# Batches 0 to 3 of an attention-and-MLP kernel: three W2 blocks cast into another tile, and sums, copies and transposes put at other places of the order

## The chip, the cores and the metric

One core of one Trainium2 chip runs the whole program. The metric is the device time of one execution in microseconds; each time is the median of several runs. Besides, one execution was taken by the hardware profiler. All times inside an execution are counted from its first instruction.

## The reference

Attention with 16 query heads over 4 key and value heads, then a residual block that mixes tokens and then channels:

```python
x  = softmax(q @ k.T / 8) @ v            # 8 batches, 16 heads, 384 tokens, 64 per head -> (8, 384, 1024)
u  = x + lam * (w_tok @ (alpha1 * x + beta1))
a2 = alpha2 * u + beta2
out = u + lam * (relu(a2 @ w_ch1) @ w_ch2)   # w_ch1 1024 x 4096, w_ch2 4096 x 1024
```

Inputs and output are float32; the kernel multiplies in bfloat16 and accumulates in float32.

## The kernel before

**Pairs.** The eight batches go through the two channel products in four pairs. Each product of a pair is done as a 2 x 2 block scheme with seven block products in place of eight, so blocks of W1, W2 and of the activations are first added or subtracted on VectorE (DVE). The operand sums of a2 lie in seven parts of one tile, `ops`; part k is `opb(k)`. Channel product one of the first pair is `first_product` (line 652, its matmuls are L692), channel product two is `second_product` (line 739, matmuls L763). The later pairs use the loops of `pair` (L842 for product one, L908 for product two).

**What sets the order.** The program is scheduled by hand: each engine executes its instructions in the order in which the Python code issues them, and so do the DMA queues of SyncE (SP) and GpSimd (POOL). A product is a generator; each `yield` ends a *step*. In product one a step is four matmuls of 384 columns, in product two four matmuls of 512 columns. The table `plan` (filled by `put(ps, second, step, function, ...)`) says which other work is issued after which step of which pair. Work that stands in the table at (0, 1, u) is issued at step u of the first pair's second product; by the count of weight loads on L763, step 8 of it begins at 137.4 us, step 23 at 155.3, step 36 at 171.4, step 40 at 176.8 and step 61 at 202.4.

**What runs beside.** While the first pair (batches 0 and 1) is in its second product, `side(2)` and `side(3)` do the attention of the next two batches: scores, exponentials, `av` (times v, divided by the sum), `tok_flip` (the token product L332, the addition L339 giving u in the tile `xr`, the product with alpha2 L342 giving a2 in one of five buffers in `obuf` that are used in turn), then `spill` (DMA of u to the output, L235) and the flip of a2 into `ops`. A *flip* is a transpose: for batch 2 `a2_transpose` (L345), a DMA transpose issued by SP into `opb(3)` or `opb(4)`; for batch 3 `turn`, on TensorE (PE) with a copy on ScalarE (ACT) into `opb(0)` or `opb(1)`. The q and k of the next batch are flipped by SP as well (L175, L171). Batches 0 and 1 go through the same stages before product one; the list near line 1182 is the end of that part, and the first steps of product one are among its entries.

**Product one of the first pair.** It goes over eight groups g in `order0` = 6, 7, 5, 4, 0, 1, 2, 3. Groups 6, 7 and 5 (`EARLY`) have a part of their products done during attention and run `SEQ0`; the others run `SEQ1`, fourteen steps (o, e) with o the block product and e one of two halves. The steps o = 1, 6, 5, 3 accumulate into the PSUM bank X[e]; after each of 1, 6, 5 an ACT copy (L700) takes a snapshot before PE adds the next. After (3, e) ACT copies a bias (L707), and DVE L709 reads the bank Y[t]; after that (4, e) may write Y[t], which L713 reads. DVE also makes the W1 sums of the next group in `sum_block` (L576 and L572), issued after four of the steps, and ACT runs `finish` (L662, a relu over the previous group's sums).

**W2 blocks.** W2 lies in quarters: "11", "12", "21", "22", each in four blocks c of 512 KB in bfloat16. A block is cast from float32 by a POOL DMA (L499); "21" is cast to DRAM and loaded by SP (L497). Blocks are held in a ring of six slots (`w1`), three slots in `pad`, or at `home(c)` in `arena`. `queue` is a list of loads; `pump` issues from its head whenever a slot comes free. After "21" is used (o = 2), its four slots take "22" c = 1 to 3 and, later, a second copy of "21" ("again") that is needed for o = 4; "again" c = 1 takes the slot of "22" c = 0 in `pad`. The first three W1 blocks of the next pair follow in the queue.

**Later pairs.** Their product one runs `SEQ1` in eight groups; `sum_w1` (L518, L523) makes the next group's sums after steps 2, 5, 8, 11.

Of the kernel before, what the change touches and what calls it, by code (L numbers as in the profile page):

```python
# [13 lines left out]
def kernel(  # L14
# [21 lines left out]
    nc = tc.nc  # L36
# [14 lines left out]
    NST = S // P  # L51
# [7 lines left out]
    RING = 6  # L59
# [63 lines left out]
    def by_tok(ap):  # L123
        return ap.rearrange("(p st) d -> p st d", st=NST)
# [97 lines left out]
    def side(b):  # L222
# [9 lines left out]
            return opb((3, 0)[b % 2] + p // 4)[:, p % 4]  # L232

        def spill(p):
            nc.sync.dma_start(out=by_tok(out[b])[:, :, cols(p)], in_=x_of(p))  # L235

        def cols(p):
            return slice(p * P, (p + 1) * P)
# [152 lines left out]
            flip(p)  # L391

        def flip(p):
            if not first:
                spill(p)
            if not by_pe(p):
                a2_transpose(p)

        def by_pe(p):
# [13 lines left out]
        at = {}  # L413
# [6 lines left out]
        for p in range(NP):  # L420
            put((4, 10, 14, 18, 24, 29, 33, 35)[p], av, p)
            put((8, 15, 17, 22, 27, 32, 36, 38 if b % 2 else 39)[p], tok_flip, p)
            if by_pe(p):
                put(((13, 20, 23, 28, 34, 37, 40, 42) if b == 3 else (0, 0, 0, 0, 0, 36, 39, 41))[p], turn, p)
        return at
# [61 lines left out]
        nc.gpsimd.dma_start(out=stored(c).rearrange("p (a c) -> p a c", a=4), in_=w2_block(name, c))  # L487

    def load_w2(name, c, slots=None):
        if slots is None:  # L490
            raw[name, c] = None, home(c)
        else:
            slot = slots.pop(0)
            raw[name, c] = slot, place(slot)
        at = raw[name, c][1]
        if name in ("21", "again"):
            nc.sync.dma_start(out=at, in_=stored(c))  # L497
        else:
            nc.gpsimd.dma_start(out=at.rearrange("p (a c) -> p a c", a=4), in_=w2_block(name, c))  # L499
# [82 lines left out]

    queue = [(load_block, kind, gp) for kind, gp in (("R1", 0), ("R2", 0), ("L1", 1), ("L2", 1), ("R1", 1), ("R2", 1))]
    queue += [(load_w2, "21", c, w1_free) for c in range(4)]
    for name, cs, slots in (("12", (0, 1), w1_free), ("12", (2, 3), pad_free), ("22", (0,), pad_free), ("22", (1, 2, 3), w1_free),
                            ("again", (0,), w1_free), ("again", (1,), pad_free), ("again", (2, 3), w1_free)):
        queue += [(load_w2, name, c, slots) for c in cs]
    queue += [(load_w1, c) for c in order1[:3]]
    for i in range(1, NB):
        heads = [(load_w1, c) for c in order1[:4]] if i + 1 < NB else []  # L590
        queue += [(load_w1, c) for c in order1[4:]] + [(fetch, i, n) for n in range(SLOTS - 2)] + heads[:2]
# [60 lines left out]
    def first_product(flush):  # L652
# [12 lines left out]
        for i, g in enumerate(order0):  # L665
            nxt = order0[i + 1] if i + 1 < len(order0) else None
            quick = g in EARLY
            snap, part_lo = {}, {}
            ts = slice(2 * g, 2 * g + 2)
            for k, (o, e) in enumerate((((7, 0), (7, 1)) if i == 0 else ()) + SEQ0 if quick else SEQ1):  # L670
                G = g
                if o == 8:
                    if nxt not in EARLY:
                        continue
                    o, G = 7, nxt
                t = 2 * G + e
                lo, hi = bias1[:, t:t + 1], bias1[:, NH + t:NH + t + 1]
                if i == 0 and (o, e) == (6, 0):
                    lead_banks.close()
                    share_banks("Z")  # L680
                if i == 0 and o == 7:
                    begin_x(t)
                if o == 1:
                    begin_x(t)
                if o == 7:
                    Ys[t] = bank([P, 512], "mm", "Y") if G == g else pairs["Z"].tile([P, 512], f32, tag="Z", name="Y", bufs=4)
                if o == 2:
                    Z = pairs["Z"].tile([P, 512], f32, tag="Z", name="Z", bufs=4)
                ps = X[e] if o in (1, 6, 5, 3) else Ys[t] if o in (7, 4) else Z
                n = S + (o in (1, 2, 5, 3))  # L690
                for dt in range(NDT // 2):
                    nc.tensor.matmul(out=ps[:, :n], lhsT=tb[G, o][:, dt, e * P:(e + 1) * P], rhs=opb(FIRST1[o], n)[:, dt],  # L692
                                     start=(o in (1, 2, 7) and dt == 0), stop=(dt == NDT // 2 - 1), skip_group_check=True)
                wide, ps = ps, ps[:, :S]
                if o in (1, 6, 5):
                    w = S + 2
                    q = ((2 if i % 2 else 8) + 2 * (1, 6, 5).index(o) + e) % 12 * w
                    n = S + (o == 1)
                    snap[o, e] = snaps[:, q:q + S]
                    nc.scalar.copy(out=snaps[:, q:q + n], in_=wide[:, :n])  # L700
                    if o == 1:
                        part_lo[e] = snaps[:, q + S:q + S + 1]
                elif o == 2:
                    tt(out=lo, in0=wide[:, S:S + 1], in1=part_lo[e], op=ADD)
                    stt(out=lead_hid[:, t, 0], in0=ps, scalar=lo, in1=snap[1, e], op0=ADD, op1=ADD)  # L705
                elif o == 3:
                    nc.scalar.copy(out=hi, in_=wide[:, S:S + 1])  # L707
                    nc.scalar.activation(out=lead_hid[:, t, 3], in_=ps, func=RELU, bias=hi)
                    stt(out=lead_hid[:, t, 1], in0=Ys[t][:, :S], scalar=hi, in1=snap[5, e], op0=ADD, op1=ADD)  # L709
                    if nxt in EARLY:  # L710
                        begin_x(2 * nxt + e)
                elif o == 4:
                    stt(out=lead_hid[:, t, 2], in0=ps, scalar=lo, in1=snap[6, e], op0=ADD, op1=ADD)  # L713
                if (o, e) in ((2, 1), (3, 1)) and i % 2:
                    free_blocks("L" if o == 2 else "R", g // 2)
                if (o, e) == (6, 0) and i == 0:
                    tt(out=opb(2), in0=opb(0), in1=opb(1), op=ADD)
                if (o, e) == (6, 1) and i == 0:
                    tt(out=opb(0), in0=opb(4), in1=opb(6), op=SUB)
                at = ((6, 0), (6, 1), (5, 0), (5, 1)) if quick else tuple(SEQ1[u] for u in (2, 5, 8, 11))  # L720
                if (o, e) in at and nxt is not None:
                    m = (5, 7, 6, 4)[at.index((o, e))]
                    sum_block(nxt, m)
                    if m == 4 and i == 0:
                        free_blocks("L", nxt // 2)
                if k == 1 and i:
                    finish(order0[i - 1])
                if (o, e) == (4, 0):
                    nc.scalar.activation(out=lead_hid[:, ts, 1], in_=lead_hid[:, ts, 1], func=RELU)
                if (o, e) == (4, 1):  # L730
                    nc.vector.tensor_scalar(out=lead_hid[:, ts, 2], in0=lead_hid[:, ts, 2], scalar1=0.0, scalar2=None,
                                            op0=mybir.AluOpType.max)
                    tt(out=lead_hid[:, ts, 2], in0=lead_hid[:, ts, 2], in1=lead_hid[:, ts, 1], op=ADD)
                yield 0
# [4 lines left out]
    def second_product(acc, later, flush, scaled):  # L739
        pad_free[:] = [RING + 1, RING, RING + 2]  # L740
        pump()
        s2, s1, s5, s3 = ([snaps[:, (NST * i + ms) * 512:(NST * i + ms + 1) * 512] for ms in range(NST)] for i in range(4))
        names = {1: "11", 2: "21", 3: "22", 5: "12", 6: "12", 7: "11", 4: "again"}
        xs_ = {}
        turns = ((1, 0), (1, 1), (2, 0), (2, 1), (1, 2), (5, 0), (2, 2), (5, 1), (5, 2),
# [11 lines left out]
        for k, (o, ms) in enumerate(turns):  # L757
# [3 lines left out]
            for t in range(NH):  # L761
# [1 line left out]
                nc.tensor.matmul(out=x, lhsT=lead_hid[:, t, FIRST2[o], ms * P:(ms + 1) * P],  # L763
                                 rhs=rhs[:, t % 4 * 512:(t % 4 + 1) * 512], start=(o in (1, 5) and t == 0), stop=(t == NH - 1),
                                 skip_group_check=True)
                if t % 4 == 3 and ms == NST - 1 and (o in (2, 3) or o == 4 and slot < RING):
                    free(slot)
                if t % 4 == 3 and t < NH - 1:
                    if t == 7 and turns[k + 1:] and turns[k + 1][0] in (3, 6, 7, 4):
# [13 lines left out]
    def pair(i):  # L783
# [45 lines left out]
        for g in range(NH // 2):  # L829
            X, Y, snap = {}, {}, {}  # L830
            for k, (o, e) in enumerate(SEQ1):
# [29 lines left out]
                    tt(out=opb(6), in0=opb(4), in1=opb(5), op=SUB)  # L861
                if k == 2 and g == 0:
                    sum_w1(0, 4)
                if k in (2, 5, 8, 11) and g + 1 < NH // 2:
                    sum_w1(g + 1, {2: 5, 5: 7, 8: 6, 11: 4}[k])
                ts = slice(2 * g, 2 * g + 2)
                if k == 1 and g:
                    finish(slice(2 * g - 2, 2 * g))
# [89 lines left out]
    with tc.manual_schedule(engines=order):  # L958
# [149 lines left out]
        for c in range(4):  # L1108
            put(0, 0, (50, 72, 74, 44)[c], load_w2, "11", c)
            put(0, 0, (6, 14, 42, 46)[c], cast_w2, "21", c)  # L1110
            put(0, 1, (41, 43, 45, 47)[c], keep_w2, 1, c)
            put(0, 1, (9, 10, 13, 15)[c], sum_w2, 5, c)
            put(0, 1, (20, 21, 25, 26)[c], sums_first_hid, 2, c)
            put(0, 1, (28, 30, 31, 34)[c], sums_first_hid, 4, c)
            put(0, 1, (37, 40, 41, 43)[c], sum_w2, 6, c)
# [6 lines left out]
        for ps in range(NB - 1):  # L1122
# [3 lines left out]
                put(ps, 0, 70 + 3 * i if ps == 0 else 91 + 2 * i, load_next, c + 1, 1)  # L1126
            put_flips(ps, 0, c, (44, 46, 50, 54, 58) if ps == 0 else range(76, 86, 2))
            put_all(ps, 1, side(c))
            for u, f, h in zip((8, 14, 14, 27, 32, 33) if ps == 0 else (10, 17, 18, 28, 33, 33),
                               (flip_q, flip_k, flip_q, flip_q, flip_k, flip_q), (0, 0, 2, 4, 2, 6)):  # L1130
                put(ps, 1, u, f, c + 1, h, 2)
            put_all(ps, 1, side(c + 1), lambda u: u + 38)
            for j, u in ((0, 77), (2, 80), (3, 83)) if ps == 0 else ((0, 76), (2, 79), (3, 81)):
# [44 lines left out]
        for i in range(36):  # L1178
            (C if i >= 18 else A).scores(i % 18)
            for f, *a in at.get(i, []):  # L1180
                f(*a)
        for f, *a in ((C.turn, 4, "sc"), (C.av, 7), (early1, 10), (C.a1, 7), (diff_first, 0, 4), (early1, 11), (C.tok, 6), (C.turn, 5, "sc"), (early2, 10),
                      (C.tok, 7), (early2, 11), (sums_first, 0, 2), (C.turn, 6, "sc"), (product, 2), (sums_first, 2, 1),
                      (C.turn, 7, "sc"), (sums_first, 3, 1), (spill_all, 1)):
            f(*a)
        for n in range(2):
            load_block(f"L{n + 1}", 0, home(n + 1))
# [36 lines left out]
```

## Time and profile before

| | us |
|---|---|
| median of 3 runs | 728.72 (728.5 to 737.16) |
| the profiled execution | 730.12 |
| its span, first to last instruction | 728.3 |
| DVE busy in the span | 550.8 (76%) |
| ACT busy | 374.0 (51%) |
| POOL busy | 190.4 (26%) |
| product one of the first pair | 58.7 to 128 |
| product two of the first pair, with attention of batches 2 and 3 | 128 to 231 |
| product one of the second pair | 231 to 305 |

The profiler's instruction rows have start, duration, engine, source line, operation, the tiles written and read, and how many like instructions were merged. Idle time of an engine is put down to what ended it (`<-`). Consecutive matmuls overlap, so a row of n matmuls lasts longer than n times the distance between their starts.

### The profile page before, as it was taken

The numbers are of one execution on the slowest core, as the hardware profiler recorded it, in microseconds if no ns is written. First come the engines' busy times: TensorE is split into PE (matmuls) and PEld (weight loads), VectorE is DVE, ScalarE is ACT, GpSimd is POOL, SyncE is SP. The second block draws the span as 40 slices with busy tenths as digits, with TensorE's granted clock in tenths as the row PEclk, the third lists the DMA queues.
The fourth block names the chain that finished last, engine by engine and source line by source line (L and its number), as shares of the span: only waits on it lengthen the run. The fifth ranks groups of instructions, "written<-read, shape, count | busy, mean of one in ns | idle before, by whom it ended". The sixth has DMA issues, their size and how long they took to land.

```text
span 728.3 us, 14356 instructions
## 1 busy us (share of the span) xinstructions
PE 711.9 (98%) x5610; PEld 406.3 (56%) x5668; DVE 550.8 (76%) x1037; ACT 374.0 (51%) x566; POOL 190.4 (26%) x242
## 2 busy tenths in 40 slices
PE   8999999999999999999999999999999999999998
PEld 5665555555555665555555566655555566654444
DVE  8888886689899877659678888748868988763354
ACT  7877666645574666644333466663433266650000
POOL 8844233120014341202122344201102222001111
PEclk9999999999999999999999999999999999999999
DMA  9999999999999999969999999999999999937975
GB/s 165 179 240 228 187 189 219 229 256 220 313 297 220 192 145 207 248 209 223 223 236 208 173 180 192 205 220 194 223 272 199 209 122 144 168 133 258 242 227 108
DMA packets 201648, 151.16 MB, mean 208 GB/s; under 512 B 90476, under 2 KB 181972, under 8 KB 201324
## 3 DMA queue, kind: packets, MB, share of 16 engines
q0 software_dynamic: 116208, 70.76, 70.8%
q1 hardware_dynamic: 84684, 79.03, 40.5%
q8 instruction: 44, 0.72, 0.4%
q10 hardware_dynamic: 688, 0.46, 0.2%
q14 instruction: 24, 0.20, 0.1%
HBM read 161.52 MB, written 37.75 MB: 274 GB/s over the span
## 4 chain that ended last, share of the span: by engine, by line
PE 80%; DVE 8%; POOL 3%; DMA 3%; issue 3%; ACT 1%; DVEq 0%; POOLq 0%; ACTq 0%
PE C L908 28%; PE X L842 14%; PE C L763 9%; PE Y L842 7%; PE sc L268 4%; PE X L692 3%; PE Z L842 3%; PE sc L303 3%; PE sc L332 3%; PE Y L692 3%; DMA w<-in_moe_w_ch_dram 2%; DMA ops<-obuf 1%; DVE pad L576 1%; PE Z L692 1%; DVE arena L705 1%
## 5 line engine op out<-in xcount | busy, mean ns | idle before, releaser
L908 PE MATMUL C<-w,arena 128*128 128x512 bf16 (+2 forms) x711 | 163.7, 372 | 1.6 <-issue 0.3
L277 ACT ACTIVATE es<-sc 128x1024 bf16<-128x1024 f32 x108 | 104.1, 1024 | 115.7 <-PE sc L268 107.4
L908 PEld LDWEIGHTS <-arena 128*128 128x128 bf16 x1040 | 94.8, 98 | 100.5 <-issue 5.1
L450 POOL DMA_DIRECT2D out_dram<-hT x45 | 39.5, 878 | 310.9 <-DVE hT L801 184.6
L847 ACT ACTIVATE hT<-X,bias 128x384 f32<-128x384 f32 x144 | 83.6, 582 | 60.2 <-PE X L842 55.4
L842 PEld LDWEIGHTS <-w 128*128 128x128 bf16 x752 | 73.6, 98 | 49.4 <-issue 0.5
L842 PEld LDWEIGHTS <-pad 128*128 128x128 bf16 x576 | 56.3, 98 | 38.0 <-issue 0.9
L842 PE MATMUL X<-ops,pad 128*128 128x384 bf16 x384 | 70.2, 326 | 0.0
L908 PE MATMUL C<-pad,arena 128*128 128x512 bf16 (+2 forms) x288 | 69.5, 373 | 0.4
L842 PE MATMUL X<-ops,w 128*128 128x384 bf16 x376 | 68.8, 326 | 0.0
L187 POOL DMA_DIRECT2D w<-in_moe_w_ch_dram x47 | 45.1, 1030 | 88.5 <-PE C L763 20.9
L332 PEld LDWEIGHTS <-wtokT 128*128 128x128 bf16 x576 | 37.5, 98 | 16.1 <-issue 3.0
L763 PEld LDWEIGHTS <-arena 128*128 128x128 bf16 x336 | 29.7, 98 | 29.8 <-issue 2.5
L849 DVE TENSOR_TENSOR arena<-Y,hT 128x384 bf16<-128x384 f32 x48 | 26.5, 557 | 20.0 <-ACT hT L847 18.0
L763 PE MATMUL C<-w,arena 128*128 128x512 bf16 x161 | 40.2, 379 | 0.4 <-issue 0.2
L339 DVE TENSOR_TENSOR xr<-sc,xr 128x384 f32<-128x384 f32 x48 | 26.4, 551 | 18.5 <-PE sc L332 18.5
L303 PEld LDWEIGHTS <-es 128*128 128x128 bf16 x864 | 32.8, 97 | 11.3
L842 PE MATMUL Z<-ops,w 128*128 128x384 bf16 x192 | 39.0, 326 | 0.0
L268 PE MATMUL sc<-qT,kT 64*128 64x384 bf16 (+2 forms) x504 | 37.2, 271 | 1.8 <-ACT hT L277 0.3
L842 PE MATMUL Y<-ops,w 128*128 128x384 bf16 x184 | 37.6, 326 | 0.3 <-DVE arena L855 0.3
L277 ACT ACTIVATE hT<-sc 128x1024 bf16<-128x1024 f32 x36 | 35.8, 1031 | 3.7 <-PE sc L268 3.6
L853 ACT ACTIVATE arena<-X,bias 128x384 bf16<-128x384 f32 x48 | 27.9, 582 | 17.7 <-PE X L842 16.1
(196 smaller groups left out, 1163.4 us busy)
## 6 DMA issues: line engine op xcount, KB each, us to landing
w<-in_moe_w_ch_dram POOLq DMA_DIRECT2D x70, 512.0 KB, 10.1
w<-w2s SPq DMA_DIRECT2D x61, 512.0 KB, 5.9
out_dram<-hT POOLq DMA_DIRECT2D x45, 256.0 KB, 6.8
pad<-w2s SPq DMA_DIRECT2D x19, 512.0 KB, 6.1
out_dram<-xr SPq DMA_DIRECT2D x48, 192.0 KB, 3.4
q_raw<-in_q_dram POOLq DMA_DIRECT2D x28, 192.0 KB, 9.9
arena<-in_moe_w_ch_dram POOLq DMA_DIRECT2D x9, 512.0 KB, 16.5
pad<-in_moe_w_ch_dram POOLq DMA_DIRECT2D x9, 512.0 KB, 12.0
```

Of the source, the lines that this page charges most:

```text
L187: nc.gpsimd.dma_start(out=w1_at[c], in_=w1src[:, :, c * CW * P:(c + 1) * CW * P])
L268: nc.tensor.matmul(out=sc[:, hh, k % 4:k % 4 + n], lhsT=kT_[r, 2 * p // G, BLK[hh][sk], :], rhs=qT_[r, p, st:st + n, :], start=True, stop= ...
L277: nc.scalar.activation(out=e, in_=sc, func=EXP, scale=scale_qk)
L303: nc.tensor.matmul(out=av[:, hh, sq, :], lhsT=ess[k // 4][:, m % 2, k % 4, :], rhs=vb[:, sk, hk, :], start=(sk == 0), stop=(sk == NST - 1))
L332: nc.tensor.matmul(out=ps[:, tt, :], lhsT=wtokT[:, st, tt * P:(tt + 1) * P], rhs=a1s[p][:, st, :], start=(st == 0), stop=(st == NST - 1 an ...
L450: nc.gpsimd.dma_start(out=by_tok(out[b])[:, ms, dw * 512:(dw + 1) * 512], in_=o, accum_op=ADD)
L692: nc.tensor.matmul(out=ps[:, :n], lhsT=tb[G, o][:, dt, e * P:(e + 1) * P], rhs=opb(FIRST1[o], n)[:, dt], start=(o in (1, 2, 7) and dt == 0 ...
L763: nc.tensor.matmul(out=x, lhsT=lead_hid[:, t, FIRST2[o], ms * P:(ms + 1) * P], rhs=rhs[:, t % 4 * 512:(t % 4 + 1) * 512], start=(o in (1, ...
L842: nc.tensor.matmul(out=ps, lhsT=tb[g, o][:, dt, e * P:(e + 1) * P], rhs=opb(LEFT1[o])[:, dt], start=(o in (1, 2, 7) and dt == 0), stop=(dt ...
L847: nc.scalar.activation(out=snap[o, e], in_=ps, func=IDENT, bias=hi if o == 5 else lo)
L853: nc.scalar.activation(out=hid[:, t, 4], in_=ps, func=RELU, bias=hi)
L908: nc.tensor.matmul(out=x, lhsT=hid[:, t, LEFT2[o], ms * P:(ms + 1) * P], rhs=rhs[:, t % 4 * 512 + c0:t % 4 * 512 + c1], start=((not last o ...
```

## The change

- `spill` of batches 2 and 3 is taken out of `tok_flip` and issued one step later; for batch 2 those of p = 4 to 7 go through POOL's queue instead of SP's.
- Batch 2's eight flips are no longer issued with `tok_flip` (steps 8, 15, 17, 22, 27, 32, 36, 39) but at steps 24, 26, 28, 29, 31, 35, 37, 40.
- The flips of batch 3's q and k move from steps 8, 14, 14, 27, 32, 33 to 23, 25, 27, 30, 33, 34.
- "22" c = 1 to 3 are cast at steps 1 to 3 into parts of `ops` that held operands of product one, and not at steps 24 to 26 into ring slots.
- "21" c = 1 to 3 stay in their ring slots until o = 4; only c = 0 is loaded a second time. The first W1 block of the next pair is loaded when "21" c = 0 is done (step 24).
- In product one of the first pair the sums 6 and 4 of the next group are issued later (in the groups of `SEQ1` after steps 10 and 13 and not 8 and 11), and `finish` in the groups 7 and 5 two steps later. In the later pairs the same two sums move in the same way.
- At the end of batch 1's attention `diff_first` (DVE L466) goes behind the seventh token product, and the first two steps of product one are split by the last `turn`.

```diff
         def spill(p):
-            nc.sync.dma_start(out=by_tok(out[b])[:, :, cols(p)], in_=x_of(p))
+            eng = nc.gpsimd if b == 2 and p > 3 else nc.sync
+            eng.dma_start(out=by_tok(out[b])[:, :, cols(p)], in_=x_of(p))
...
         def flip(p):
-            if not first:
+            if b > 3:
                 spill(p)
-            if not by_pe(p):
+            if b != 2 and not by_pe(p):
                 a2_transpose(p)
...
             put((8, 15, 17, 22, 27, 32, 36, 38 if b % 2 else 39)[p], tok_flip, p)
+            if b < 4:
+                put((9, 16, 18, 23, 28, 33, 37, 39 if b % 2 else 40)[p], spill, p)
+            if b == 2:
+                put((24, 26, 28, 29, 31, 35, 37, 40)[p], a2_transpose, p)
...
     def load_w2(name, c, slots=None):
-        if slots is None:
+        if name == "22" and c:
+            raw[name, c] = None, ops[:, (0, 0, 2048, 5 * BE)[c]:][:, :2048]
+        elif slots is None:
             raw[name, c] = None, home(c)
...
-    for name, cs, slots in (("12", (0, 1), w1_free), ("12", (2, 3), pad_free), ("22", (0,), pad_free), ("22", (1, 2, 3), w1_free),
-                            ("again", (0,), w1_free), ("again", (1,), pad_free), ("again", (2, 3), w1_free)):
+    for name, cs, slots in (("12", (0, 1), w1_free), ("12", (2, 3), pad_free), ("22", (0,), pad_free)):
         queue += [(load_w2, name, c, slots) for c in cs]
-    queue += [(load_w1, c) for c in order1[:3]]
+    queue += [(load_w1, order1[0]), (load_w2, "again", 0, pad_free), *((load_w1, c) for c in order1[1:3])]
...
-                at = ((6, 0), (6, 1), (5, 0), (5, 1)) if quick else tuple(SEQ1[u] for u in (2, 5, 8, 11))
+                at = ((6, 0), (6, 1), (5, 0) if nxt in EARLY else (3, 1), (3, 1) if nxt in EARLY else (4, 1)) if quick else tuple(
+                    SEQ1[u] for u in (2, 5, 10, 13))
...
-                if k == 1 and i:
+                if (o, e) == ((5, 1) if quick else (1, 1)) and i:
                     finish(order0[i - 1])
...
+        raw.update((("again", c), raw["21", c]) for c in range(1, 4))
...
-                if t % 4 == 3 and ms == NST - 1 and (o in (2, 3) or o == 4 and slot < RING):
+                if t % 4 == 3 and ms == NST - 1 and slot is not None and (
+                        o == 2 and t == 3 or o == 3 or o == 4 and slot < RING):
                     free(slot)
...
-                if k in (2, 5, 8, 11) and g + 1 < NH // 2:
-                    sum_w1(g + 1, {2: 5, 5: 7, 8: 6, 11: 4}[k])
+                if k in (2, 5, 10, 13) and g + 1 < NH // 2:
+                    sum_w1(g + 1, {2: 5, 5: 7, 10: 6, 13: 4}[k])
...
+            if c:
+                put(0, 1, c, load_w2, "22", c)
...
-            for u, f, h in zip((8, 14, 14, 27, 32, 33) if ps == 0 else (10, 17, 18, 28, 33, 33),
-                               (flip_q, flip_k, flip_q, flip_q, flip_k, flip_q), (0, 0, 2, 4, 2, 6)):
+            for u, f, h in (((23, flip_q, 0), (25, flip_k, 0), (27, flip_q, 2), (30, flip_q, 4), (33, flip_k, 2), (34, flip_q, 6))
+                            if ps == 0 else
+                            ((10, flip_q, 0), (17, flip_k, 0), (18, flip_q, 2), (28, flip_q, 4), (33, flip_k, 2), (33, flip_q, 6))):
                 put(ps, 1, u, f, c + 1, h, 2)
...
-        for f, *a in ((C.turn, 4, "sc"), (C.av, 7), (early1, 10), (C.a1, 7), (diff_first, 0, 4), (early1, 11), (C.tok, 6), (C.turn, 5, "sc"), (early2, 10),
-                      (C.tok, 7), (early2, 11), (sums_first, 0, 2), (C.turn, 6, "sc"), (product, 2), (sums_first, 2, 1),
-                      (C.turn, 7, "sc"), (sums_first, 3, 1), (spill_all, 1)):
+        for f, *a in ((C.turn, 4, "sc"), (C.av, 7), (early1, 10), (C.a1, 7), (early1, 11), (C.tok, 6), (diff_first, 0, 4), (C.turn, 5, "sc"), (early2, 10),
+                      (C.tok, 7), (early2, 11), (sums_first, 0, 2), (C.turn, 6, "sc"), (product,), (sums_first, 2, 1),
+                      (C.turn, 7, "sc"), (product,), (sums_first, 3, 1), (spill_all, 1)):
             f(*a)
```

## The prediction, made before the changed kernel was run

> **What bounds the kernel now.** The page's busy table and clock come first:
>
> ```profile
> PE 711.9 (98%) x5610; PEld 406.3 (56%) x5668; DVE 550.8 (76%) x1037; ACT 374.0 (51%) x566; POOL 190.4 (26%) x242
> PEclk9999999999999999999999999999999999999999
> ```
>
> PE sets the time, at full clock. The change removes no matmul, so it can win only idle time of PE: 728.3 - 711.9 = 16.4 us in the span, of which windows show 4.5 us before 60 us and 3.6 us after 700. Next, PE's waits between 57 and 282 us, where everything that is moved lies (total us, times, longest; one row, on L332 at 222 us, is left to F):
>
> ```profile
> PE tp L406 <- DVE obuf L342: 0.7, 1, 0.7
> PE X L692 <- ACT hT L700: 0.6, 2, 0.3
> PE X L692 <- DVE ops L462: 0.5, 1, 0.5
> PE Y L842 <- DVE arena L849: 0.5, 1, 0.5
> PE Y L692 <- DVE arena L709: 0.4, 1, 0.4
> PE Y L692 <- DVE arena L713: 0.4, 2, 0.2
> PE Y L842 <- DVE arena L855: 0.3, 1, 0.3
> ```
>
> No row is a wait for a W2 block or a flip; they are PSUM handovers in product one and its first operands. This understates the loss: matmuls start 0.163 us apart (eight in 1.30 us in the chain) but a row shows 0.33 us for one, so I count each loss as start minus the start due at that pace. PE's timeline where attention ends:
>
> ```profile
> 57.05 0.82 PE L624 MATMUL E<-ops,w 128*128 128x385 bf16 x4
> 58.53 0.34 PE L406 MATMUL tp<-ident,obuf 128*128 128x128 bf16 x3 [0.67 <-DVE obuf L342]
> ...
> 60.18 0.65 PE L692 MATMUL X<-ops,pad 128*128 128x384 bf16 x3
> 61.30 2.00 PE L692 MATMUL X<-ops,pad 128*128 128x384 bf16 x10 [0.47 <-DVE ops L462]
> ```
>
> The transpose was due at 57.05 + 4 x 0.163 = 57.70 and came at 58.53 (0.83 lost); the fourth X matmul was due at 60.67 and came at 61.30 (0.63 lost). In a `SEQ1` group DVE's timeline, then PE's:
>
> ```profile
> 97.41 0.68 DVE L576 TENSOR_TENSOR pad<-w,pad 128x1024 bf16<-128x1024 bf16 x1
> 98.01 1.14 DVE L709 SCALAR_TENSOR_TENSOR arena<-Y,bias,hT 128x384 bf16<-128x384 f32 x2
> ...
> 100.39 0.68 DVE L576 TENSOR_TENSOR pad<-arena,pad 128x1024 bf16<-128x1024 bf16 x1
> 100.99 1.13 DVE L713 SCALAR_TENSOR_TENSOR arena<-Y,bias,hT 128x384 bf16<-128x384 f32 x2
> ```
>
> ```profile
> 97.71 0.82 PE L692 MATMUL Z<-ops,arena 128*128 128x385 bf16 x4
> 98.67 1.46 PE L692 MATMUL Y<-ops,pad 128*128 128x384 bf16 x8
> 99.97 1.47 PE L692 MATMUL X<-ops,arena 128*128 128x385 bf16 x8
> 101.66 0.81 PE L692 MATMUL Y<-ops,w 128*128 128x384 bf16 x4 [0.22 <-DVE arena L713]
> ```
>
> A W1 sum (0.68) stands on DVE ahead of both evacuations of Y. PE's Y was due at 98.36 and 101.28: 0.31 and 0.38 lost.
>
> **The parts and their sum.**
>
> *A, end of attention.* `diff_first` (0.96 us on DVE from 56.39, held by flips until then) stands before L339 and L342 of the seventh token product. Behind them, L339 starts when L326 ends (55.82) and L342 ends at 57.00, so the 0.83 goes. `diff_first` then runs 56.95 to 57.9, the last L342 ends at 59.0, as now 59.6. PE makes one step of product one to 58.5, waits for that L342 (0.5 lost, new), and turns by 59.2. ACT's copy takes 0.48 after about 0.2, the last quarter of `sums_first` 0.36: 60.3. PE has by then done the second step and three X matmuls (59.85 to 60.34). The fourth comes at 60.34 for 61.30: 0.95 won. Bounds: 0 (flips late, `diff_first` holding the last pair) to both losses, 1.46.
>
> *B, `finish` two steps later.* The ACT relu (0.85) stands between snapshots; PE lost 0.59 at 70.81 (sixteen matmuls from 67.61 due to end at 70.22), the same at 77.91, and 0.60 at 79.82. Moved, it stands before L707 and so before L709, which frees Y. In group 7 two other steps lie between, and about 0.15 comes back at the second half: 0.27 won. In group 5 none do: after (3,0) ends, ACT is still 0.75 in `finish`, then L707 0.16 and L709 0.61, and (4,0) starts 0.95 late where it was 0.60; with the earlier 0.5 gone 0.05 is left. Together 0.3; bounds -0.3 and 1.4.
>
> *C, sums 6 and 4 behind the evacuations in `SEQ1`.* The Y loss recurs at 89.25, 98.67, 108.47 and 118.26 (0.30 each), the other at 101.66 and 111.44 (0.38). By the new order L709 starts some 0.55 earlier and L713 0.6; both losses go: 1.95. DVE's work in a group stays (7.4 of 9.1 us: four sums 2.7, L704 with L705 1.5, L709 and L713 2.3, L731 and L733 0.9), and sum 6 is needed seven steps, 4.5 us, later. Lower bound 1.2, the first kind alone.
>
> *D, second pair.* After L523 has waited 3.0 us for a W1 block at 274.65, PE loses 0.62 at 276.59 (behind L849, ahead of which nothing changes) and 0.46 at 279.65 (behind L855; sum 4 now follows it): 0.46 won, bounds 0 and 1.08. Sum 6 in the later pairs passes only steps that ACT evacuates, so DVE's order is the same there: nothing. After sum 4 come L872 and L874, 0.6 later, which nobody waits for within the group.
>
> *E, the W2 blocks.* Three casts of 0.78 us on POOL move from 158 to about 131 us, ahead of the store at 145.64 that waits 14.10 us for DVE: hidden. By the trace these casts land in order, the last ones at 140.56, 143.08 and 146.20, so the three would land near 149, 151.5 and 154; they are needed at step 36 (171.4). The "12" sums start at 140.50, 141.64, 145.26, 148.47 on blocks that landed at 135.43, 137.96, 140.56, 143.08; product one being 3.2 us shorter (A + B + C), the smallest margin is 0.5 us. Three SP loads of 512 KB go; what used them begins after step 61. Nothing won, nothing lost; without the margin, up to 1 us.
>
> *F, spills and flips.* SP's spills one step later free `xr` for an `av` at least 13 steps after. The four on POOL cost some 0.9 us each there (as its stores, L450) and pass the third store and the next W1 load, whose sums wait until step 77: nothing. The loss of 0.89 at 222.23 (DVE full) stays; were it to go, 0.9 more.
>
> Sum: 0.95 + 0.3 + 1.95 + 0.46 = 3.7. The span goes from 728.3 to 724.6, the profiled execution from 730.12 to 726.4; the median is 1.4 below the profiled one: 728.72 - 3.7 = **725.0 us**. All lower bounds with E's loss: 0.1 better than now; all upper ones: 6.7 won, 722.
>
> **The rivals.** *Burst of flips, slower.* Fourteen DMA transposes are now issued by SP in steps 23 to 40, 21.5 us, where they were spread over 40. SP's rows:
>
> ```profile
> 163.90 1.24 SPq L345 DMA_TRANSPOSE ops<-obuf  x1
> 165.19 4.97 SPq L175 DMA_TRANSPOSE qT<-q_raw  x1
> ```
>
> The fourteen of now sum to 25.2 us, 1.8 each; the long one stands beside three casts. The five at 80 to 103 us, beside casts too, took 4.5 on average, 5.6 at most. A late flip holds its `obuf` buffer, and DVE's L342 five uses on waits, with PE behind it. With m us a flip, the twelfth (batch 2's sixth) lands at 155.3 + 12m + 4; its buffer is wanted at 199.65. The wait is 12m - 40: none at 1.8, the whole gain at 3.7, and 2% lost at 4.9 (18.6 - 3.7 = 14.9: 744 us). Against it: two of the three casts beside these flips are gone, and a W1 block takes the place of the third. Batch 3's scores (step 38) wait for the first and third flip only. Chance 0.10, of which 0.07 over 2%.
>
> The Trainium skill's page "Advanced Engine Details and Errata", section "X-Bar Transpose (TRN2)", says that transpose DMAs run as fast as regular ones, 350 to 400 GB/s: the 2 MB of this burst would be an estimated 6 us, and the rival could not occur. The trace's 25 us on SP disagree, so I keep its chance.
>
> *Nothing gained.* The handovers form again: `finish` in group 5, the new wait in A, DVE late on a "12" block, DVE full at 215 to 235 whatever came before. With A at 0, B at -0.3, E at -1 and half of C: about 728.5. For it: DVE is 76% busy overall, 88.6 of 103 us in this product two. Chance 0.20.
>
> *The moves do not do what they say.* Where the engine's order stays (sum 6 above), nothing; were C's losses due to ACT's bias copy and not to the sum, 1.95 goes: 727.0. Against it: L709 starts as the sum ends (97.41 + 0.6), the bias being copied by 97.42. Inside the forecast's range.
>
> **How the numbers follow.** Forecast 0.69 (722 to 727.5), nothing gained 0.20, burst 0.10, more than all upper bounds 0.01. The range 722 to 731 holds forecast, nothing gained and the burst's small cases. Over 2% (14.6 us, about what a measurement of this kernel can tell from no change) faster needs nearly all idle time of the span, start and tail too: 0.01. Slower by that is the burst with m over 4.9: 0.07. Within: 0.92.
>
> **What would show it.** A: the fourth X matmul follows the third; a wait for L342 before the last turn. B: no L700 wait at 70 and 77, a longer L709 one before (4,0) of group 5. C: no L709 or L713 waits from 85 to 120. D: no L855 wait near 276. E: no SP loads of "again" but one, casts at 131. Burst: SP transposes over 3.7 us and DVE L342 waiting for a DMA. Wrong if PE waits in product two of the first pair for L763 blocks or `qT`.

## The result and the profile after

The changed kernel takes 735.59 us (median of 21 runs, 729.4 to 752.01) where the kernel before takes 729.9 (21 runs beside them, 728.5 to 737.16): ratio 1.006, 95% interval 1.0034 to 1.0086. It is 0.6% slower; 725.0 had been forecast. Medians are of all runs; ratios leave out runs more than 1.5% above the fastest of their kernel (two of the 21 here, four of ten in e9). The profiled execution took 738.84 us, its span 737.1 against 728.3.

The page of the changed kernel, busy table, clock and DMA rows:

```profile
PE 720.4 (98%) x5668; PEld 407.5 (55%) x5668; DVE 551.7 (75%) x1037; ACT 374.1 (51%) x566; POOL 193.6 (26%) x246
...
PEclk9999999999999999999999899999999999999999
DMA  9999999999899999969999999999999999937975
```

TensorE is busy longer for the same work, in part because the clock is no longer full (one slice shows 8), in part because the trace of before holds 58 matmul records fewer for the same 5668 weight loads. So the 16.4 us of idle time that the prediction began from are too many. The DMA row is the one that the prediction never read. In the kernel before it says nearly the same:

```profile
DMA  9999999999999999969999999999999999937975
```

The DMA engines are at 90% or more in 35 of 40 slices before and in 34 after: a second thing that is busy nearly always, beside TensorE's 98%. The row does not single out a stretch; it says 9 in product one as well.

TensorE's waits from 57 to 282 us after the change, the same view as the first of the prediction (total us, times, longest):

```profile
PE sc L333 <- DVE a L322: 3.1, 2, 2.4
PE Y L698 <- DVE arena L715: 0.6, 1, 0.6
PE sc L407 <- ACT es L278: 0.2, 1, 0.2
PE tp L407 <- DVE obuf L343: 0.2, 1, 0.2
PE Y L698 <- DVE arena L719: 0.2, 1, 0.2
```

Lines are now 1 to 9 higher (L692 is L698, L763 is L771, L342 is L343). The seven small handovers of before are nearly gone, and one wait of 2.4 us is new. It begins on VectorE, shown here with SyncE's queue (start, us, engine, line, what):

```profile
166.68 0.55 DVE L340 TENSOR_TENSOR xr<-sc,xr 128x384 f32<-128x384 f32 x1
170.72 0.56 DVE L343 TENSOR_TENSOR obuf<-xr,vecs 128x384 bf16<-128x384 f32 x1 [3.49 <-DMA ops<-obuf]
```

```profile
155.06 1.80 SPq L175 DMA_TRANSPOSE qT<-q_raw  x1
157.40 4.60 SPq L346 DMA_TRANSPOSE ops<-obuf  x1
162.19 2.55 SPq L171 DMA_TRANSPOSE kT<-k  x1
```

L343 writes the sixth of batch 2's `a2` tiles into the buffer of the first, whose flip SyncE issued at 157.40 and which landed at 170.63, 13.2 us later. TensorE's stage there, by windows of 4 us (PE, PEld, DVE, ACT, POOL busy, then clock, DMA share, GB/s; the share adds up the times of all packets, so it can pass 1):

```profile
168.00:172.00 4.00, 2.84 (x29) 1.40 (x27) 1.22 (x3) 1.69 (x3) 0.29 (x1) 1.00 1.35 194
172.00:176.00 4.00, 2.78 (x14) 1.44 (x15) 3.85 (x8) 0.00 (x0) 0.00 (x0) 0.69 1.22 208
176.00:180.00 4.00, 4.00 (x32) 1.97 (x31) 2.50 (x4) 2.33 (x3) 0.71 (x1) 0.88 0.74 156
```

After the wait the granted clock falls: eight L771 matmuls take 3.41 us where eight usually take 1.89. The shares of 0.69 and 0.88 come to some 3.4 us at half clock. The wait cost 2.55 us, the lowered clock 1.7 more.

I set the two traces side by side at the same weight load (5668 in both). The changed kernel starts even (+0.07 at 52 us), wins 0.96 at the end of attention, 0.48 up to 81 us and 1.21 up to 131, loses 4.23 between 165 and 185, wins 0.81 at 276 to 280 and loses 7.93 at 402 us, in the second pair's product two: 8.8 in all. The last loss is a wait for a W2 block, again with a lowered clock behind it (some 6.8 us at half, by windows of 4 us):

```profile
PE C L917 <- DMA w<-w2s: 4.8, 1, 4.8
```

### The profile page after: what moved, and what is told of

Its sections match the earlier page's. It is cut to its first block, busy times and chain, and to the rows that moved or that the text cites. A ratio compares the mean times of both kernels' runs of the same rounds, so it can differ in the third digit from the quotient of the medians.

```text
span 737.1 us, 14408 instructions
## 1 busy us (share of the span) xinstructions
PE 720.4 (98%) x5668; PEld 407.5 (55%) x5668; DVE 551.7 (75%) x1037; ACT 374.1 (51%) x566; POOL 193.6 (26%) x246
## 4 chain that ended last, share of the span: by engine, by line
PE 80%; DMA 7%; DVE 5%; issue 3%; POOL 3%; ACT 1%; POOLq 0%; ACTq 0%; DVEq 0%
PE C L917 29%; PE X L851 13%; PE C L771 7%; PE Y L851 7%; PE X L698 4%; PE sc L269 4%; PE Z L851 3%; DMA w<-in_moe_w_ch_dram 3%; PE sc L304 3%; PE sc L333 3%; PE Y L698 2%; DMA w<-w2s 2%; DMA ops<-obuf 2%; PE E L630 1%; PE tok L333 1%
## 5 line engine op out<-in xcount | busy, mean ns | idle before, releaser
L917 PE MATMUL C<-w,arena 128*128 128x512 bf16 (+2 forms) x744 | 171.2, 377 | 4.8 <-DMA w<-w2s 4.8
L917 PEld LDWEIGHTS <-arena 128*128 128x128 bf16 x1040 | 95.4, 98 | 107.3 <-issue 13.2
L771 PEld LDWEIGHTS <-arena 128*128 128x128 bf16 x336 | 30.2, 99 | 30.8 <-issue 4.2
L333 PE MATMUL sc<-a,wtokT 128*128 128x128 bf16 x432 | 32.2, 220 | 3.1 <-DVE a L322 3.1
```

The source lines that it names most:

```text
L333: nc.tensor.matmul(out=ps[:, tt, :], lhsT=wtokT[:, st, tt * P:(tt + 1) * P], rhs=a1s[p][:, st, :], start=(st == 0), stop=(st == NST - 1 an ...
L917: nc.tensor.matmul(out=x, lhsT=hid[:, t, LEFT2[o], ms * P:(ms + 1) * P], rhs=rhs[:, t % 4 * 512 + c0:t % 4 * 512 + c1], start=((not last o ...
```

## The experiments

The theory after the result: in the stretch from 130 to 185 us transfers land only just in time, because the DMA engines are loaded; whatever comes earlier there, or is added there, waits for a transfer. The rival: one part of the change (early casts, late flips, the reordering) is at fault by itself. All ratios are to the kernel before, run on the same chip. A variant has ten runs where nothing else is said; times inside an execution come from the one profiled.

### The parts alone (e1 to e4)

The diff is cut in three: the reordering (A to D), the early casts with the reused "21" blocks (E), and the new places of flips and spills (F). e1 has the first; e2 adds the casts, e3 the flips; e4 has casts and flips without the reordering.

> Only the reordering (W1 sums behind evacuations, `finish` later, the new order at the end of attention); casts, spills and flips as before. Theory (the loss comes from flips and casts alone): the 2.6 us won up to the start of product two and the 0.8 won at 276-280 us stay won: 3.4 us under the kernel before (ratio 0.995), mean clock 1.000, no wait of TensorE over 1 us at 165-180 or at 400 us. Rival (being earlier uses up margins that casts and flips had): a wait of 2 us or more appears in product two of a pair, clock under 0.998, ratio 1.000 or more.

Measured: 731.09 us, ratio 1.0006 (0.9971 to 1.0042). The trace has 2.38 us won at 131 us, all of it lost again and 5.4 more by 185. VectorE's waits for DMA from 130 to 215 us:

```profile
DVE xr L311 <- DMA out_dram<-xr: 5.4, 3, 3.4
```

L311 needs an `xr` tile whose spill lies in SyncE's queue behind slow transposes:

```profile
144.64 3.32 SPq L171 DMA_TRANSPOSE kT<-k  x1
148.01 6.82 SPq L175 DMA_TRANSPOSE qT<-q_raw  x1
...
162.12 5.20 SPq L345 DMA_TRANSPOSE ops<-obuf  x1
...
168.71 4.23 SPq L345 DMA_TRANSPOSE ops<-obuf  x1
```

In the kernel before the first two took 1.31 and 2.17. The rival named for e1 holds: with casts and flips untouched, only being earlier turns the margin (the time by which a transfer lands ahead of its use) into a wait.

> The reordering and the early raw casts; batch 2's flips and spills and batch 3's q and k flips at their old steps. If the flips' places make the loss: flip of the first head pair of batch 2 is issued near 146 and lands by 158, needed at 167, so no wait of VectorE for it: ratio 0.995. If the casts' crowding of the DMA engines makes it: flips of 4 to 5 us each beside the casts (now at steps 8 to 17, 143 to 153 us), a wait for a flip or a block of 2 us or more between 150 and 180 us, ratio 1.000 to 1.006.

Measured: 740.92 us (4 runs), ratio 1.0135 (1.0045 to 1.0225). The flips of k and q beside the casts took 7.52 and 8.36 us, and L311 waited for a spill (`out_dram<-xr`) 9.4 us, until 172.6.

> The reordering and the new places of flips and spills; raw W2 casts and the reloads of the sums as before (three casts near 158 us, three reloads). If the flips' places make the loss: VectorE waits 3 us or more for the first flip of batch 2 near 167-171, TensorE 2.5 us, then about 3.6 us of lowered clock: 4.2 us back, ratio 1.001. If the early casts make it: the flip issued at 157 lands within 6 us, no wait there, ratio 0.995.

Measured: 732.07 us, ratio 1.0021 (0.9982 to 1.006). No wait at 170 (the obuf wait is 0.7 us in all), 2.02 us still won at 196; then 2.8 lost between 202 and 209, where VectorE's sums wait for blocks that are still being stored:

```profile
DVE arena L512 <- DMA w2s<-arena: 2.7, 2, 1.4
```

> Everything but the reordering: casts, spills and flips new, product one and the later pairs' sums as before. Theory (casts and flips cost 4.2 us at 170, the reordering gives 3.4): ratio 1.006 without a wait at 400 us, 1.016 with one. If the wait at 400 us comes of the later pairs' sums placed later, it is absent here: no wait over 2 us for a W2 block in the second pair's product two. If it comes of casts and flips, it is there as in the changed kernel (4.8 us, then 3 us of lowered clock).

Measured: 736.77 us, ratio 1.0055 (1.0006 to 1.0104). Its profile waits 2.9 us at the step that falls near 170 in the changed kernel; no W2 wait at 402, but a 2.7 us wait for `q_raw` at 28 us, ahead of all edits. Each part makes a wait, and each at another transfer (spill, flip, store): that is the theory's side, but not yet a proof.

### Less and more to move (e5, e6)

e5 leaves out three accumulating stores, so its output lacks one partial product; e6 adds a cast whose result is not used.

```diff
# e5: the reordering, and
     def store(b, ms, dw, o):
+        if len(skipped) < 3:
+            skipped.append(ms)
+            return
# e6: the kernel before, and at step 1 of product two
+        nc.gpsimd.dma_start(out=ops[:, :2048].rearrange("p (a c) -> p a c", a=4), in_=w2_block("22", 1))
```

> The reordering alone, with the three accumulating stores of product two's first quarter (256 KB each, issued near 143, 149 and 163 us) left out, so that one partial product is missing from batch 0's output; VectorE's scalings stay. New theory (product two between 130 and 185 us is paced by the DMA engines, which are over 90% busy and hold 10 to 15 us of backlog; TensorE's earlier arrival is only turned into a wait): with less to move, flips and spills land earlier, no wait of VectorE for a spill or flip over 1 us, the 2.4 us stay won after 190 us, ratio 0.996 and 3 us or more under the reordering alone. Rival (a transpose on SyncE's queue is slow by itself wherever it falls): transposes of 4 to 7 us remain, ratio 1.000.

> The kernel before with one more cast of a raw W2 block (512 KB written, into the dead operand tile, read by nobody) at step 1 of product two; nothing else moved. DMA theory: transfers behind it land 3 us later, the kernel before has 1 to 3 us of margin, so 1 to 6 us are lost at 150 to 185 us: ratio 1.002 to 1.008, clock under 1.000 in most runs. Rival (before has ample margin, and the loss in the changed kernel comes of its order of flips): ratio 1.000 within 0.002.

Measured: e5 726.8 us, 8 of 10 runs between 726.42 and 728.65, ratio 0.9957 (0.9918 to 0.9996); e6 735.62 us, ratio 1.0063 (1.0024 to 1.0102). In e5 VectorE waits for no DMA from 130 to 215 us, and what the reordering won is kept to the end. SyncE's queue there, for the transposes shown above of e1:

```profile
145.47 1.53 SPq L171 DMA_TRANSPOSE kT<-k  x1
147.04 2.48 SPq L175 DMA_TRANSPOSE qT<-q_raw  x1
...
156.22 1.24 SPq L345 DMA_TRANSPOSE ops<-obuf  x1
...
162.34 1.29 SPq L345 DMA_TRANSPOSE ops<-obuf  x1
163.68 4.05 SPq L175 DMA_TRANSPOSE qT<-q_raw  x1
```

Same order, same instructions: 0.75 MB less in POOL's queue takes 6.82 to 2.48, 5.20 to 1.24 and 4.23 to 1.29. One transpose beside the casts of 157 to 159 us still takes 4.05 (3.16 in e1), now with nothing waiting behind it. In e6, with nothing reordered, one cast that nobody reads slows the same transpose of q (2.17 in the kernel before) and makes L311 wait:

```profile
148.99 7.76 SPq L175 DMA_TRANSPOSE qT<-q_raw  x1
```

```profile
DVE xr L311 <- DMA out_dram<-xr: 3.6, 2, 3.3
```

and the kernel before loses 4.8 us by 185. So the theory holds in both directions: less to move takes the waits away, more brings them, the order of SyncE's queue being the same. The rival (transposes slow wherever they fall) falls but for that one. What slows a transpose is not shown beyond this: between 140 and 190 us of before, e1 and e6, windows of 10 us with DMA shares of 0.87 to 1.35 moved 177 to 345 GB/s, so the share is no measure of a full rate.

### The same bytes at another time (e7 to e11)

e7 and e8 hold the three accumulating stores back (`later[0][1] == 1 and k > 8`); e9 to e11 hold the second pair's first W1 load, and what stands behind it in `queue`, until POOL has passed step 52's place in its order:

```diff
+            if f == load_w1 and held:
+                return
...
+        put(0, 1, 52, let_go)
```

> The changed kernel with the first pair's first three accumulating stores held back to steps 36, 38 and 40 of product two (about 171 to 176 us), where DMA has room behind; the bytes are the same. DMA theory: 1.5 MB of reads and writes go from the crowded stretch into one where DMA is 60 to 90% busy; the first flip of batch 2 lands 4 to 6 us earlier (by 166), the 2.5 us wait at 170 and its lowered clock go: ratio 0.998 to 1.001. If flips are slow because of the casts alone: no change, ratio 1.006.

Measured: 731.82 us, ratio 1.0016 (0.998 to 1.0051). The wait near 170 remains at 3.1 us on VectorE (1.8 lost), then 1.0 more is lost at 175: smaller, not gone. Its profile also waits 5.5 us for a W2 block at 573.

> The reordering and the new places of flips and spills, W2 loads as before, with the same three stores held back to steps 36 to 40. DMA theory: no wait over 1 us up to 200 us, and the waits for the kept sums at 202 to 209 us (2.8 us in all) stay or grow by up to 2 us, since the stores now share the engines with those: ratio 0.996 to 1.002. If the later stretch is not DMA's: ratio 0.996.

Measured: 733.96 us, ratio 1.0046 (1.0015 to 1.0076). Clear to 190, then a sum waits 3.3 us for a stored block at 194: the bytes only moved the wait.

> The changed kernel with the W1 loads for the second pair held back until step 52 of product two (about 190 us; one of them, 1 MB read and 512 KB written, is issued at 155.8 us and lands at 171.2 in the changed kernel, and is needed after 225 us). DMA theory: the transfers behind it land about 3 us earlier, so the wait for the first flip of batch 2 (2.55 us at 170, with the lowered clock 4.2) shrinks by 2 to 4 us: 728 us in runs without a late W2 wait, ratio 0.998 to 1.002. If the flip is late because of the three early casts and the stores ahead of it alone: 731 as before, ratio 1.005.

Measured: 735.47 us, ratio 1.0015 (0.9976 to 1.0054). The load went at 176.75, not at 190: POOL takes it as soon as its queue reaches it. The mechanism came true: no wait for a flip, 2.62 us won at 131 and still 2.62 at 246. The time did not, because of later waits (from 390 to 600 us):

```profile
PE C L925 <- DMA w<-w2s: 3.9, 2, 2.6
PE Y L859 <- DVE arena L866: 1.3, 1, 1.3
PE sc L269 <- DVE xr L340: 1.3, 1, 1.3
```

> The same with the three accumulating stores held to steps 36, 38, 40 as well. DMA theory: both free the stretch, no wait over 1 us from 140 to 200 us, and the change keeps what it won: 725.5 to 727 us in most runs, ratio 0.996. If the stores then collide with the kept sums near 185 to 205 us: a wait of 1 to 4 us there, ratio 0.999 to 1.003.

Measured: 735.52 us, ratio 1.0021 (0.9975 to 1.0067); 1.7 lost by 203 behind a sum that waited 1.5 us for a kept block: the collision of the last sentence. The 725.5 to 727 us did not come; its lowest run is 727.98. The profile lost more ahead of all edits, at 28 to 34 us:

```profile
PE sc L269 <- DMA arena<-q_raw: 6.5, 1, 6.5
```

> The reordering and the new places of flips and spills, W2 loads as before, W1 loads held until step 52. DMA theory: the waits for the kept sums' transfers at 202 to 209 us (2.8 us) vanish or shrink below 1 us, since up to three W1 blocks leave that queue: ratio 0.996 to 0.998, most runs 726 to 728. If they come of the kept sums alone: unchanged, ratio 1.002.

Measured: 731.27 us, ratio 1.0002 (0.9968 to 1.0036); the waits for kept sums stay (2.5 us): they do not come of the W1 loads, and the ratio of 0.996 to 0.998 did not come.

### Which losses are fixed (e12, e15, e16)

> The changed kernel once more, for a second profile. If its losses are fixed parts of its schedule: the wait near 170 us (2.5 us and lowered clock) and the wait for a W2 block at 402 us (4.8 us and lowered clock) both stand there again. If the later wait is one of chance (transfers late by luck of the DMA engines): the wait near 170 is there again, the one at 402 is gone or stands at another block of a later pair, and runs divide into some near 731 and some near 737.

> A further profile of the changed kernel. The wait near 170 us of 2 to 5 us with the lowered clock behind it is there; a wait of over 2 us for a W2 block in a later pair is there in about half of such profiles if it is of chance, at 402 or 574 us.

> A further profile of the kernel before. If the later waits for W2 blocks are the DMA engines' chance in every version, margins at 402 and 574 us are small here too (blocks land less than 4 us ahead of their use, or in one of a few profiles too late); if they are the change's own, the blocks land 4 us or more ahead.

Measured: 733.11 us for e12 (ratio 1.0025, 0.999 to 1.006), 735.47 for e15, 728.71 for e16 (one run each; e12 and e15 are the changed kernel, e16 the kernel before). The wait near 170 stands in all three profiles of the changed kernel, on VectorE 3.5, 4.0 and 5.7 us; e15's row:

```profile
DVE obuf L343 <- DMA ops<-obuf: 5.7, 1, 5.7
```

That part is the schedule's own: 4.2, 4.4 and 6.9 us with the lowered clock, which takes the 2.4 to 2.6 won back and more. The wait at 402 is in one of the three only; in e12 and e15 a smaller one stands at 442 to 446 us. In e16 this W2 block lands at 393.06 and the next at 394.31, 6.2 and 5.8 us ahead of their use; in the first profile of before the two have 4.8 and 4.3 us, in e12 and e15 4.8 to 5.8. By e16's expectation margins of 4 us and more say that the late block is the change's own, but e12 and e15 have them too: why it was late in the one profile stays open. e16 also lacks the losses of 276 to 280 us, as do e4 and e6, all without the later sums: they belonged to a late W1 block of the one execution that I had read.

### Casts in a quieter place, and the late waits (e13, e14, e17, e18)

```diff
-                put(0, 1, c, load_w2, "22", c)
+                put(0, 1, 16 + 2 * c, load_w2, "22", c)
```

> As the changed kernel with held W1 loads, and the three early casts of raw W2 blocks moved from steps 1 to 3 to steps 18, 20 and 22 of product two (behind the first two accumulating stores, about 150 us). DMA theory: stores and kept sums land as early as in the kernel before, the casts by 168; no wait over 1 us up to 200 us, first 300 us 3.5 us shorter than before's. If late waits in the later pairs come of chance, 3 to 6 runs of 10 still have them (735 to 740) and the rest lie at 726 to 728; if they come of the crowded stretch, 8 of 10 lie at 726 to 728.

> The same with spills and flips of batches 2 and 3 at their old places. DMA theory: as the early casts are gone from 135 to 150 us, the flips at 139 to 150 take 1.2 to 2.5 us again and the spills follow: no wait of 8 us as with early casts; but the casts at 150 fall beside the flips at 150 to 165, so a wait of 0 to 3 us at 165 to 178: ratio 0.996 to 1.002. If early or late casts are the same to the flips: 737 or more.

Measured: e13 730.84 us (726.6 to 740.74), ratio 1.0003 (0.9959 to 1.0047); e14 737.24 us (4 runs), ratio 1.0119 (1.0063 to 1.0176), with a wait of 9.8 us for a spill at 164 to 174. In e13 the stretch up to 300 us is clear, 3.24 us shorter than in the first profile of before (1.8 shorter than in e16, which lacks 1.4 of that without any edit); its later waits give 4.4 back:

```profile
PE C L925 <- DMA w<-w2s: 2.5, 2, 1.8
PE Y L859 <- DVE arena L866: 0.9, 1, 0.9
```

Four of its ten runs lie at 726.6 to 728.6, the others at 730.4 and above: nearer to what the expectation said for chance, which is not shown by that. e14's 9.8 us say that casts may not share their stretch with flips that have spills behind them: e13 needs its late flips.

> As e13 (casts at steps 18 to 22, flips and spills late, W1 loads held) but without the reordering, so that product two is reached when the kernel before reaches it. If the late waits in later pairs go with the early casts (and the sum blocks that stay in place instead of being loaded again): mean clock at or under 0.996 in 4 of 10 runs or more, as in e9, e10 and e13. If they go with being 2.4 us early: 1 or 2 of 10 as in the kernel before; the other runs at 728 to 729.

> The kernel before with only the new places of flips and spills and the held W1 loads; no early casts, no reordering. Late waits with the casts: clock at or under 0.996 in 1 or 2 of 10 runs. Late waits with flips or held loads: 4 of 10. The waits for kept sums at 202 to 209 us (2.5 us in e3 and e11) shrink below 1 us if they come of the early arrival, ratio 1.000; they stay if they come of the flips' places, ratio 1.003.

Measured: e17 730.21 us, ratio 0.9966 (0.9925 to 1.0006), mean clock at or under 0.996 in 2 of 14 runs; e18 734.19 us, ratio 1.0018 (0.9974 to 1.0061), 2 of 12, the waits for kept sums at 207 to 211 us still there, so of the flips' places; its lowest run is 732.34 against 728.71 of before, so the late flips without the casts lose too. So a low mean clock does not go with the casts as such.

A mean clock that low marks long waits, though not where they are. It stands in 17 of 123 runs of before beside e1 to e18 (none of 13 on the chip of e13, 6 of 23 on that of e17), 12 of 21 of the changed kernel (15 of 32 with e12 and e15), 6 of 10 of e9 and of e10, 3 of 10 of e13, 2 of 10 of e5. In the profiles that have it the waits are of several kinds: near 170 (the changed kernel, e4, e15), for spills (e1, e2, e14), for W2 blocks (e7, e11) and, in e10 and e17, 6.5 and 6.4 us for `q_raw` ahead of all edits. W2 blocks are waited for without the casts too (4.6 us at 578 in e18). So the counts cannot tell late waits from early ones, and why long waits come more often in some versions stays open. No version with the whole output is shown to beat the kernel before; the lowest run of e13 is 726.6, of before 728.5.

## Why the prediction was wrong

*The step that failed* is the price of transfers in E and F. E charged nothing to what shares the DMA engines with the early casts ("nothing lost, hidden"), and F's rival let a flip land 4 us after its issue; the first flip of batch 2 landed after 13.2 us, and VectorE and TensorE waited for it. That place lost 4.2 to 6.9 us in three profiles, more than the 2.4 to 2.6 won ahead of it; the rest of the 5.7 us between the medians lies in later waits, whose cause stays open.

*What bounds the kernel.* "PE sets the time" was half of it: an idle-time sum of TensorE holds only where transfers have room. The engine rows do not show that, nor does the DMA row alone: it says 9 through product one, where 2.4 us were won, and through product two, where they were lost. Landing times show it.

*A* came out as forecast, 0.95 and 0.96, and the new wait for L343 before the last turn is there (0.23). But most of its size was luck: of the loss that it takes away, 0.61 is absent in e6, e16 and e18, which keep the old order. There `diff_first` was not held by a flip, as it was in the one execution that I had read; the rows are of before and of e16:

```profile
56.39 0.96 DVE L466 TENSOR_TENSOR ops<-ops 128x1536 bf16<-128x1536 bf16 x1 [0.57 <-DMA ops<-obuf]
```

```profile
55.98 0.95 DVE L466 TENSOR_TENSOR ops<-ops 128x1536 bf16<-128x1536 bf16 x1
```

Against these three the new order is worth 0.35.

*B and C* were partly right: 2.25 forecast, 1.69 measured. B's own figures give 0.44 (0.59 less 0.15) and 0.24 (0.59 and 0.60 less 0.95) for its two groups, not 0.27 and 0.05; 0.35 and 0.12 came, about 0.5, with the longer wait before group 5's (4,0) as forecast (0.80 lost where 0.95 was said). C gave 1.2 for 1.95, its lower bound. Timeline of TensorE after, the group that the prediction showed:

```profile
96.75 1.46 PE L698 MATMUL Y<-ops,pad 128*128 128x384 bf16 x8
98.06 1.47 PE L698 MATMUL X<-ops,arena 128*128 128x385 bf16 x8
99.68 0.81 PE L698 MATMUL Y<-ops,w 128*128 128x384 bf16 x4 [0.16 <-DVE arena L719]
```

The first kind of loss (four of 0.30) is gone to 0.1; the second is 0.32 and 0.26 for 0.38 each, since in the group shown a shuffle of L1057 (0.72) and L711 (0.62) still stand before L719.

*D* was wrong: nothing. The 0.46, and 0.6 beside it, vanish in executions that keep the old order.

*E* failed in its times. The casts were said to land at 149, 151.5 and 154, with the 2.5 us spacing of the last "12" casts; they landed at 154.93, 158.58 and 162.34, 3.7 us each. "Nothing lost, hidden" was then wrong for what came behind: the store issued at 143.06 landed at 165.4 (22 us; the one issued at 145.64 before had taken 8.5), and the flips slowed.

*F and the burst.* The mechanism of the rival (a late flip holds its `obuf` buffer, L342 waits, TensorE behind it) is what happened, in three profiles of three. Its two signs came as well, a transpose over 3.7 us (4.60) and L343 waiting for a DMA. Its size failed: I priced a landing at 4 us after the issue and so put the deciding point at the twelfth flip, with no wait below 3.3 us a flip. The fourteen transposes took 27.4 us of SyncE's queue, 2.0 each, so that point was not reached. The first flip of batch 2 landed 13.2 us after its issue, and the wait came there, at the second of the fourteen. The trace of before already had a landing of 6.8 us in this stretch (the flip issued at 152.69). With 157.40 + 13.2 against a need at 167.2, 3.4 us follow from the rival's own sum. "Two of the three casts beside these flips are gone" spoke against it; they had only been moved into the backlog ahead of them. The W1 block that takes the place of the third counts as well: in e9, which holds it back, this wait is gone.

*The missing term.* No wait was charged for the clock. After 2.38 us of waiting TensorE ran at half rate for some 3.4 us; the 4.8 us wait at 402 cost 7.9. The Trainium skill's page "TensorE: Matmul & The Clock Gate", Part 1 on the clock gate, says that the clock falls to half after an idle window of about 3.4 us and comes back after as long a stretch of work. The half rate and its length agree with the trace (some 3.4 us after the first wait, twice that after the second); the wait that brought it was shorter here, 2.38 us, and e13's two waits of 1.8 and 0.7 us brought none (its mean clock is 1.000).

*The transposes.* The estimate of 6 us for the burst, from the Trainium skill's page "Advanced Engine Details and Errata", X-Bar Transpose, stands against the 27.4 us that the fourteen held SyncE's queue: a flip of 96 KB 1.20 us at least (82 GB/s) and 4.60 at most in this stretch, 5.20 in e1. A flip of q, 192 KB, took 1.24 at least, so this time is not one of bytes alone; it depends on what else is under way.

*The sums.* The lower bounds (0, -0.3, 1.2, 0 and E's -1) add up to 0.1 worse than now, and not to 0.1 better.

## What to carry to other kernels

Where transfers land just before they are needed, moving work earlier buys only a wait unless bytes leave that stretch too. e5 against e1 (three transfers less, some 4 us) and e6 (one transfer more, a wait with nothing moved) are the tests that tell it; a DMA row of 9 beside a full TensorE is a reason to make them, and no more. Price a moved transfer by the time from issue to landing under the load that it will meet, and charge its delay to everything in the same and the neighbouring queue. Take an idle time for a gain only when a second execution shows it too: most of A and all of D fall by that. Add the lowered clock to every wait above some 2 us; in these profiles single waits of 1.8 us and less brought none.

## What was not expected of the hardware

A transpose issued by SyncE holds that queue longer when other transfers are under way: between 130 and 185 us a flip of 96 KB took 1.20 to 5.20 us, one of q (L175, 192 KB) 1.24 to 8.36, and the spills behind waited with it. The three early casts of 512 KB blocks, issued 0.7 us apart, landed 3.7 us apart. The waits of 2.4 and 4.8 us in the changed kernel's first profile cost TensorE 1.7 and 2.9 us more by the lowered clock.
